# Three early loads change places on two DMA queues of a cross-network kernel

## The chip, the cores and the metric

The kernel runs on one core of a Trainium2 chip. The metric is device time in microseconds of one execution, as the median of several runs. TensorE (PE) does matmuls and loads their weights (PEld), VectorE (DVE), ScalarE (ACT) and GpSimd (POOL) do the rest, and SyncE (SP) only issues DMAs here. DMAs are issued on a queue of the engine that issues them, and the transfers of all queues run on the same 16 DMA engines.

## The reference

Six cross layers on 4096 rows of 416 features (26 fields of 16), all in bf16:

```python
def setup_inputs():
    B, F, D, L = 4096, 26, 16, 6
    Din = min(F * D, 1024)
    return {
        "x0": _w((lambda *s: _rng.normal(s) * 0.05)(B, Din)),
        "ws": _w((lambda *s: _rng.normal(s) * 0.05)(L, Din, Din)),
        "bs": _w((lambda *s: _rng.normal(s) * 0.05)(L, Din)),
    }

def reference(x0, ws, bs):
    x = x0
    for l in range(ws.shape[0]):
        x = x0 * (x @ ws[l] + bs[l]) + x
    return x
```

## The kernel before

**Tiling.** The 416 features are three chunks of 128 (`CH`, index c or m for outputs, k for inputs) and a tail of 32. The 4096 rows are four blocks of 1024 (`SB`, index s), each of two halves of 512 (`H`, index h). Data stand with features on partitions and rows along the free dimension: `x0T_sb` holds the three chunks of x0, `x0t_sb` the tails, where four groups of 256 rows lie on four groups of 32 partitions. The loop at L583 goes over blocks, then layers; `main` (L327) does four matmuls of 32 output columns each for one output chunk m and one input chunk k, `tail_rows` and `tail_outs` (L343, L385) the tail's part, and DVE (L455) adds the bias and multiplies with x0.

**The order of work.** A small planner (`Plan`) keeps one list of operations for each engine in the order in which the code adds them. From the names that an operation reads and writes it derives the semaphore waits. Nothing is reordered: each engine and each DMA queue runs its list in order. A DMA's `writes` key is what later operations wait for.

**The beginning.** The first half of block 0 doesn't come through a transposing DMA. Rows 0 to 511 are loaded as they lie (`load_rows`, two loads of 208 KB into `xin_sb`), turned on TensorE (`turn_rows`, L542) and copied by DVE to `x0T_sb` (L552). TensorE runs 12 filler matmuls (`fill`, L303) before that. Rows 512 to 1023 come through a transposing DMA (`load_transposed(0, H, SB)`, L211), which brings the three chunks but not their tails. The tail inputs of these rows are a load of their own: `xtl_sb`, four groups of 128 rows with 32 features, 64 bytes for each piece, 32 KB in all. `tail_in` (L402) turns the tails of all 1024 rows on TensorE, from `xin_sb` and `xtl_sb`; ACT (L416) and DVE (L420) copy them to `x0t_sb`.

**The weights of layer 0** are three separate loads, one for each input chunk k (104 KB each), so that `main` for k=0 waits only for the first (`weights`, L321). The tail weights of layer 0 are loaded once (26 KB) and replicated on chip (`replicate`, L278). For the later layers `load_main` brings all three chunks in one DMA.

**The first half's first layer** is the one place where the code interleaves by input chunk:

```python
                    for k in CH:
                        for part in range(2) if k == 0 else (None,):
                            for m in CH:
                                main(s, l, 0, m, k, part)
                        if k == 1:
                            tail_in()
                            bias_sums()
                    tail_rows(s, l, True)
```

So TensorE needs, in this order: the rows of `xin_sb`, W0's first chunk, W0's second chunk, the tail inputs, the biases, W0's third chunk, the replicated tail weights, and then the transposed rows 512 to 1023 for h=1.

**The queues before.** SyncE: rows, rows, W0 second chunk, W0 third chunk, transposing load, W1, tail weights of layer 1 (four DMAs), W2 and so on. ScalarE: tail weights of layer 0, W0 first chunk, tail inputs; after these three its compute begins. GpSimd: the biases.

Of the kernel before, what the change touches and what calls it, by code (L numbers as in the profile page):

```python
# [118 lines left out]
def bass_standalone__dcn_v2_cross__recsys_kernel(  # L119
# [6 lines left out]
    B, D = x0.shape  # L126
    L = ws.shape[0]
    NC = 3
    DF = 128 * NC
# [6 lines left out]
    JS = SB // 128  # L136
# [3 lines left out]
    CH = range(NC)  # L140

    with ExitStack() as es:

        def sb(name, shape, dt=BF16):
            return es.enter_context(nc.sbuf_tensor(name, shape, dt))
# [5 lines left out]
        xtl_sb = sb("xtl_sb", [128, JS, DR])  # L151
# [28 lines left out]
        x0_v = x0.rearrange("(j p) d -> p j d", p=128)  # L180
# [6 lines left out]
        def quad(q):  # L187
            return slice(32 * q, 32 * q + 32)
# [5 lines left out]
        def load(queue, dst, src, name, writes):  # L194
            P.add(queue, lambda e: e.dma_start(dst, src), writes=writes, dma=name)
# [13 lines left out]
        def load_transposed(s, a, b):  # L209
            P.add(  # L210
                "sync", lambda e: e.dma_start_transpose(x0T_sb[:, :, s * SB + a:s * SB + b], x0[s * SB + a:s * SB + b, 0:DF]),  # L211
                writes=[("x0T", s, c, h) for c in CH for h in HALVES if a <= h * H < b], dma="x0T%d" % s,
            )
# [21 lines left out]
        load_rows("sync", 0)  # L235
        load_rows("sync", 1)
        load("scalar", wt_sb[quad(0), 0, :], ws[0, DF:D, :], "wt0", [("wtq",)])
        for k in CH:
            queue = "sync" if k else "scalar"
            load(queue, w_sb[:, 0, k, :], ws[0, 128 * k:128 * k + 128, :], "w0_%d" % k, [("w", 0, k)])  # L240
        load("scalar", xtl_sb[:, 4:JS, :], x0_v[:, 4:JS, DF:D], "xtl0", [("xtl", 0)])
        load_transposed(0, H, SB)
        load_main(1)
        load_tail_weights(1, 2, "wt1")
# [548 lines left out]
```

## Time and profile before

| what | us |
|---|---|
| median of 3 runs | 127.68 |
| lowest, highest run | 127.36, 127.82 |
| profiled execution, its own time | 128.1 |
| span of the profiled execution, first to last instruction | 126.8 |
| PE busy | 123.6 (97% of the span) |
| PE weight loads busy | 64.6 (51%) |
| DVE busy | 100.0 (79%) |
| ACT, POOL busy | 43.0 (34%), 41.0 (32%) |

The page gives the busy time of each engine, the chain of work that ended last, the costliest groups of instructions, and the DMA issues with their time to landing. "Q" behind an engine's name (SPq, ACTq) marks the issue of a DMA by that engine's sequencer. Matmuls are pipelined, and a group's busy time says little of what one costs; the distance between the starts of successive groups says more. "x4" at the end of a line means four instructions merged into it.

### The profile page before, as it was taken

How to read it: one execution, taken by the hardware profiler on the slowest of the kernel's cores; microseconds unless marked ns; L12 is line 12 of the kernel's file. 1: busy time of each engine (PE TensorE's matmuls, PEld its weight loads, DVE VectorE, ACT ScalarE, POOL GpSimd, SP SyncE). 2: the span in 40 equal slices, each digit the busy share in tenths (PEclk: the TensorE clock that was granted, in tenths of full speed). 3: DMA queues.
4: the chain of work that ended last, by engine and by line, in shares of the span. 5: the costliest groups of instructions: out<-in, count | busy, mean ns of one | idle time of the engine just before them, and what ended most of it. 6: DMA issues, size and time to landing. Idle time of an engine off the chain costs nothing.

```text
span 126.8 us, 5226 instructions
## 1 busy us (share of the span) xinstructions
PE 123.6 (97%) x2373; PEld 64.6 (51%) x2373; DVE 100.0 (79%) x157; ACT 43.0 (34%) x94; POOL 41.0 (32%) x84
## 2 busy tenths in 40 slices
PE   7999999999999999999999999999999999999992
PEld 5654555555545545545545545555555455455561
DVE  2449779779779779788798797797797797797974
ACT  3324225225205225234213242252222252252910
POOL 6505324134014044053122142251320440543590
DMA  3995999010039596107019695107007990070107
GB/s 108 254 253 157 308 158 158 25 25 0 8 83 130 115 213 70 36 16 274 0 32 207 115 163 99 31 16 252 22 0 173 108 292 5 14 255 10 31 20 249
DMA packets 35013, 14.21 MB, mean 112 GB/s; under 512 B 26186, under 2 KB 34992, under 8 KB 34992
## 3 DMA queue, kind: packets, MB, share of 16 engines
q1 hardware_dynamic: 33536, 13.19, 48.4%
q10 hardware_dynamic: 1424, 0.70, 1.9%
q8 instruction: 18, 0.29, 1.0%
q14 instruction: 3, 0.02, 0.1%
q0 software_dynamic: 32, 0.01, 0.0%
HBM read 3.89 MB, written 3.41 MB: 58 GB/s over the span
## 4 chain that ended last, share of the span: by engine, by line
PE 97%; DVE 0%; issue 0%
PE ps L295 94%; PE ps L303 2%; PE ps L542 1%; DVE o_sb L718 0%
## 5 line engine op out<-in xcount | busy, mean ns | idle before, releaser
L455 DVE SCALAR_TENSOR_TENSOR xT_sb<-ps,cb_sb,x0T_sb 128x512 bf16<-128x512 f32 x114 | 76.8, 743 | 15.6 <-PE ps L295 15.6
L295 PE MATMUL ps<-xT_sb,w_sb 128*32 128x512 bf16 (+1 forms) x1596 | 84.2, 364 | 0.0
L295 PEld LDWEIGHTS ps<-xT_sb,w_sb 128*32 128x32 bf16 x1596 | 40.9, 97 | 37.2 <-issue 4.0
L465 ACT ACTIVATE t_sb<-ps,cb_sb 64x256 f32<-64x256 f32 x46 | 21.6, 470 | 57.2 <-PE ps L295 56.9
L478 POOL TENSOR_TENSOR xt_sb<-t_sb,x0t_sb 128x256 bf16<-128x256 f32 x20 | 13.4, 672 | 66.6 <-ACT t_sb L465 66.6
L430 ACT ACTIVATE xt_sb<-xt_sb 32x256 bf16<-32x256 bf16 x38 | 15.7, 414 | 15.1 <-POOL xt_sb L478 14.9
L295 PE MATMUL ps<-x0T_sb,w_sb 128*32 128x512 bf16 (+1 forms) x348 | 19.2, 369 | 0.0
L432 POOL COPY xt_sb<-xt_sb 32x256 bf16<-32x256 bf16 x38 | 14.9, 393 | 2.4
L455 DVE SCALAR_TENSOR_TENSOR xo_sb<-ps,cb_sb,x0T_sb 128x512 bf16<-128x512 f32 x18 | 12.1, 743 | 2.5 <-PE ps L295 2.5
L295 PEld LDWEIGHTS ps<-x0T_sb,w_sb 128*32 128x32 bf16 x348 | 9.1, 101 | 7.7 <-issue 1.1
L295 PE MATMUL ps<-xt_sb,wt_sb 32*128 32x512 bf16 (+1 forms) x152 | 11.6, 326 | 0.0
L295 PE MATMUL ps<-xt_sb,wc_sb 32*128 32x256 bf16 x76 | 7.3, 268 | 0.0
L295 PEld LDWEIGHTS ps<-xt_sb,wt_sb 32*128 32x128 bf16 x152 | 2.3, 91 | 8.1 <-DVE xT_sb L455 8.1
L478 POOL TENSOR_TENSOR xot_sb<-t_sb,x0t_sb 128x256 bf16<-128x256 f32 x3 | 2.0, 672 | 9.9 <-ACT t_sb L465 9.9
L295 PE MATMUL ps<-w_sb,xT_sb 128*32 128x416 bf16 (+1 forms) x60 | 5.0, 339 | 0.0
L442 DVE SCALAR_TENSOR_TENSOR xT_sb<-ps,cb_sb,x0T_sb 128x512 bf16<-128x512 f32 x6 | 4.0, 744 | 0.8 <-PE ps L295 0.8
L718 DVE TENSOR_TENSOR o_sb<-ps,xr_sb 128x416 bf16<-128x416 f32 x7 | 3.7, 583 | 0.8 <-PE ps L295 0.8
L295 PEld LDWEIGHTS ps<-xt_sb,wc_sb 32*128 32x128 bf16 x76 | 3.9, 93 | 0.2
L303 PE MATMUL ps<-const-bfloat16-1.0 128*128 128x256 bf16 x12 | 2.7, 417 | 0.8 <-PEq L778 0.8
L552 DVE COPY x0T_sb<-ps 128x256 bf16<-128x256 bf16 x6 | 1.4, 292 | 2.2 <-PE ps L542 2.2
L295 PEld LDWEIGHTS ps<-w_sb,xT_sb 128*32 128x32 bf16 (+1 forms) x60 | 2.3, 97 | 1.2
L488 ACT ACTIVATE sS_sb<-ps,cb_sb 128x384 bf16<-128x384 f32 (+1 forms) x5 | 2.7, 629 | 0.0
(48 smaller groups left out, 32.3 us busy)
## 6 DMA issues: line engine op xcount, KB each, us to landing
out_dram<-o_sb SPq DMA_DIRECT2D x2, 832.0 KB, 4.8
w_sb<-in_ws_dram SPq DMA_DIRECT2D x5, 312.0 KB, 3.9
out_dram<-o_sb SPq DMA_DIRECT2D x2, 416.0 KB, 3.2
xr_sb<-in_x_dram SPq DMA_DIRECT2D x1, 832.0 KB, 5.0
xin_sb<-in_x_dram SPq DMA_DIRECT2D x2, 208.0 KB, 2.8
wt_sb<-in_ws_dram SPq DMA_DIRECT2D x4, 104.0 KB, 3.3
out_dram<-o_sb ACTq DMA_DIRECT2D x3, 104.0 KB, 1.9
out_dram<-o_sb SPq DMA_DIRECT2D x3, 104.0 KB, 1.7
```

What stands on the lines that cost most here:

```text
L295: return pe.matmul(dst, lhsT=lhsT, rhs=rhs, start=start, stop=True, skip_group_check=True, tile_position=pos,)
L303: ins = pe.matmul(ps[:, 7, 0:256], lhsT=const[:, 0:128], rhs=const, start=True, stop=True)
L430: fn = lambda e, d=dst, s=src: e.activation(out=d, in_=s, func=ACTF.Copy)
L432: fn = lambda e, d=dst, s=src: e.tensor_copy(out=d, in_=s)
L442: "vector", lambda e: e.scalar_tensor_tensor(out=xj[:, js, c, :], in0=ps[:, bank(h, c), :].rearrange("p (j f) -> p j f", f=128), scalar=cb ...
L455: "vector", lambda e: e.scalar_tensor_tensor(out=dst, in0=ps[:, bank(h, c), :], scalar=cb_sb[:, c, l:l + 1], in1=x0T_sb[:, c, o:o + H], op ...
L465: "scalar", lambda e, p=p, h=h: e.activation(out=dst[p, :], in_=ps[p, T_BANK[h], 0:G], func=ACTF.Identity, bias=cb_sb[p, NC, l:l + 1]), re ...
L478: "gpsimd", lambda e: e.tensor_tensor(out=dst, in0=t, in1=x0t_sb[:, s, 0, :], op=ALU.mult),
L488: fn = lambda e: e.activation(out=o, in_=i, func=ACTF.Identity, bias=b)
L542: ins = pe.transpose(out=psT[:, b, j * 128:(j + 1) * 128], in_=xin_sb[:, 2 * i + j, c * 128:(c + 1) * 128], identity=ident[:, :],)
L552: "vector", lambda e, d=dst, s=src: e.tensor_copy(out=d, in_=s),
L718: "vector", lambda e: e.tensor_tensor(out=o_sb[:, jj, :], in0=ps[:, b, 0:D], in1=xr_sb[:, j, :], op=ALU.mult), reads=[("ps", b), ("xr",)], ...
```

## The change

The tail inputs go from the third place of ScalarE's queue to the third of SyncE's. W0's third chunk goes from the fourth place of SyncE's queue to the third of ScalarE's, and W0's second chunk from the third place of SyncE's to the fourth. The order after it:

| place | SyncE before | SyncE after | ScalarE before | ScalarE after |
|---|---|---|---|---|
| 1 | rows 0-255 | rows 0-255 | tail weights 0 | tail weights 0 |
| 2 | rows 256-511 | rows 256-511 | W0 first chunk | W0 first chunk |
| 3 | W0 second chunk | tail inputs | tail inputs | W0 third chunk |
| 4 | W0 third chunk | W0 second chunk | | |
| 5 | transposing load | transposing load | | |

```diff
@@ -235,10 +235,9 @@
         load_rows("sync", 0)
         load_rows("sync", 1)
         load("scalar", wt_sb[quad(0), 0, :], ws[0, DF:D, :], "wt0", [("wtq",)])
-        for k in CH:
-            queue = "sync" if k else "scalar"
+        load("sync", xtl_sb[:, 4:JS, :], x0_v[:, 4:JS, DF:D], "xtl0", [("xtl", 0)])
+        for k, queue in ((0, "scalar"), (2, "scalar"), (1, "sync")):
             load(queue, w_sb[:, 0, k, :], ws[0, 128 * k:128 * k + 128, :], "w0_%d" % k, [("w", 0, k)])
-        load("scalar", xtl_sb[:, 4:JS, :], x0_v[:, 4:JS, DF:D], "xtl0", [("xtl", 0)])
         load_transposed(0, H, SB)
         load_main(1)
         load_tail_weights(1, 2, "wt1")
```

The number of loads, their sizes and every instruction of the other engines stay as they are.

## The prediction

> **What bounds the kernel now.** I read the chain of waits first. It shows whether a transfer ends anything on the path that sets the end.
>
> ```profile
> 7 pieces in order of time: start us, us, what
> 0.79 0.04 issue
> 0.83 2.72 PE ps L303 x12
> 3.56 0.01 issue
> 3.57 1.50 PE ps L542 x12
> 5.06 119.42 PE ps L295 x2248
> 124.49 0.02 issue
> 124.51 0.59 DVE o_sb L718
> ```
>
> From 0.83 to 124.49 us the chain never leaves TensorE (PE). No DMA is a piece of it. Filler matmuls (L303) run until the first rows land, the turning of the rows (L542) until 5.06, and after that matmul follows matmul. A moved load can change the end only by making TensorE wait where it doesn't now, or by ending a wait that it has.
>
> Second, the timeline of the first 9 us, for the queues that the change touches. Columns: start, duration, engine, line, operation.
>
> ```profile
> 0.80 0.87 SPq L195 DMA_DIRECT2D xin_sb<-in_x_dram  x2
> ...
> 1.25 0.45 ACTq L195 DMA_DIRECT2D w_sb<-in_ws_dram  x1
> ...
> 1.71 0.91 SPq L195 DMA_DIRECT2D w_sb<-in_ws_dram  x2
> 1.72 0.46 ACTq L195 DMA_DIRECT2D xtl_sb<-in_x_dram  x1
> ...
> 2.66 1.64 SPq L211 DMA_TRANSPOSE x0T_sb<-in_x_dram  x1
> ```
>
> The third and fourth places of SyncE's queue are issued at 1.71 and (by a closer look) 2.19 us, the third of ScalarE's at 1.72. Third, the DMA issues one window at a time, whose last figure is the time from issue to landing; I add it to the issue.
>
> ```profile
> w_sb<-in_ws_dram SPq DMA_DIRECT2D x1, 104.0 KB, 3.1
> xtl_sb<-in_x_dram ACTq DMA_DIRECT2D x1, 32.0 KB, 4.3
> ...
> w_sb<-in_ws_dram SPq DMA_DIRECT2D x1, 104.0 KB, 3.7
> x0T_sb<-in_x_dram SPq DMA_TRANSPOSE x1, 4.6
> ```
>
> So W0's second chunk (w0_1) lands at 1.71 + 3.1 = 4.8 us, the tail inputs (xtl) at 1.72 + 4.3 = 6.0, W0's third chunk (w0_2) at 2.19 + 3.7 = 5.9, the transposed rows 512 to 1023 at 2.66 + 4.6 = 7.3. Last, narrow timelines of TensorE, for when each is first wanted.
>
> ```profile
> 6.04 0.16 PEld L295 LDWEIGHTS ps<-x0T_sb,w_sb 128*32 128x32 bf16 x4
> ...
> 6.25 0.56 PE L295 MATMUL ps<-x0T_sb,w_sb 128*32 128x512 bf16 x4
> ...
> 6.64 0.38 PE L295 MATMUL ps<-x0T_sb,w_sb 128*32 128x512 bf16 x4
> ...
> 6.86 0.10 PEld L295 LDWEIGHTS ps<-ident,xtl_sb 128*32 128x32 bf16 x2
> ...
> 7.38 0.34 PEld L295 LDWEIGHTS ps<-x0T_sb,w_sb 128*32 128x32 bf16 x12
> ...
> 8.69 0.34 PEld L295 LDWEIGHTS ps<-x0T_sb,w_sb 128*32 128x32 bf16 x16 [0.21 <-issue]
> ```
>
> These are the weights for k=1 (6.04, first matmul 6.25), `tail_in` (6.86), k=2 (7.38), and the second half of the rows (8.69). The slack today is 6.04 - 4.8 = 1.2 us for w0_1, 6.86 - 6.0 = 0.8 for xtl, 7.38 - 5.9 = 1.5 for w0_2, and 8.69 - 7.3 = 1.4 for the transposed rows. None of the four is late, so there is nothing to win from landing one earlier.
>
> **The change, part by part.** No instruction is added or removed; three of eight early loads change places.
>
> *Issue time.* SyncE issues xtl (0.46 us, from ScalarE's row) where it issued a weight chunk (0.43). What stands behind it there is the transposing load at 2.66, then w1 at 4.35 and the later weights: each 0.03 us later, with 1.4 us of slack at the transposing load and 10.76 - (4.35 + 3.9) = 2.5 us at w1, whose first use is the loading of xT weights at 10.76. Without that cover it would cost 0.03 us. ScalarE issues a chunk in 0.45 in place of 0.46; behind it stand its table load (2.21) and the replica of the tail weights (3.72), wanted at 8.14. Cost: 0.
>
> *Tail inputs, third on SyncE.* They take the place from which w0_1 landed at 4.8. They are 32 KB against 104, but in 64-byte pieces. ScalarE's queue moved 622 packets, most of them these, in the window 3.5 to 7.3 for 14.8% of 16 engines, i.e. 0.148 x 3.8 = 0.56 us for each engine; that is the most they can hold up one engine. Landing between 4.8 and 4.8 + 0.56 = 5.4; I take 5.0. Wanted at 6.86, as now. Gain 0, since TensorE has no wait there.
>
> *W0's third chunk, third on ScalarE.* Issue 1.72. Bounds: 1.72 + 3.1 = 4.8 (a chunk's quickest) and 1.72 + 4.3 = 6.0 (the place's own figure today). Wanted at 7.38, so at least 1.4 us of slack. Cost 0.
>
> *W0's second chunk, fourth on SyncE.* This is the one load that comes closer to its use. Issue about 2.19. Lower bound: 2.19 + 3.1 = 5.3. Next: 2.19 + 3.7 = 5.9, what the fourth place gave w0_2. Upper bound: 2.19 + 4.3 = 6.5, the slowest of these loads. Against 5.9 speaks that its queue now holds 208 + 208 + 32 = 448 KB ahead of it, where w0_2 had 520, and that no small packets run beside it by then. Estimate from third place plus the small packets: 4.8 + 0.56 = 5.4. I take 5.5, between these two and nearer the lower. That leaves 6.04 - 5.5 = 0.5 us to the weight load and 0.7 to the matmul. Cost 0; from a landing of about 6.1 on it costs what it is late. At 6.5 the first matmul starts near 6.5 + 0.15 (one weight load), 0.4 us late. TensorE's in-order work behind that wait is all there is: `tail_in`, the bias sums, k=2, tail rows.
>
> The Trainium skill, "DMA: Bandwidth & Descriptors", section Queues, rings and completion order, says that on each engine a queue's descriptors are taken in order while the queues that have work alternate. By that rule w0_1 waits for all the small tail pieces and w0_2 runs beside them; the sum would still be 0, with the landing at 5.4 rather than 5.9.
>
> *The transposing load.* The same bytes stand ahead of it on the 16 engines, in the same number of SyncE issues; 7.3 plus or minus 0.3 (the gap between the two estimates above), wanted at 8.69. Cost 0.
>
> *TensorE's only early wait for a load* is on the second pair of rows, issued at 1.26, ahead of everything that moves. It lands about 1.26 + 2.9 = 4.2, and turning resumes then. What runs beside its last packets is the end of W0's first chunk in both kernels. Bound either way: 0.06 us, the break between the two runs of six turning matmuls.
>
> **Sum.** 0.0 us, from -0.06 to +0.4 on these rows without what follows below. Against the profiled execution: span 126.8, its own time 128.1, so 1.3 us lie around the span; both stay. That execution is 0.4 us above the median 127.68 of the three runs, so I forecast the median itself and not 128.1: **127.65 us**.
>
> **Rivals.**
> (a) *Slower: w0_1 comes late and the fast matmul rate with it.* The rows above show that groups of 512 columns start 0.39 us apart from 6.25 to 6.64 and 0.22 apart from 6.64 to 6.86; before that, groups of 256 columns start 0.21 apart (5.61 and 5.82 in a closer look). TensorE ran at about half rate until some 6.6 us, although the windows show a granted clock of 1.00 throughout. If w0_1 lands after 6.1, TensorE idles shortly before that step. Had the step needed the 3.0 us of work since its last wait (3.57 to 6.6) and to start over, it would cost 0.4 + 3.0/2 = 1.9 us: 129.6. If the step keeps its time, only 0.2 to 0.4: 127.9 to 128.1. For it: 5.9, the fourth place's landing, is only 0.2 from the deciding point. Against: the bytes ahead are fewer, and the idle stretch is short. The Trainium skill, "TensorE: Matmul & The Clock Gate", Part 1, ties the step to a busy window of about 3.4 us; by it a spoilt window would cost up to 3.4/2 = 1.7 us on top of the stall, 129.8. The trace agrees with a step in rate, not yet with any window.
> (b) *Faster: the profile flatters the old order.* xtl has the least slack, 0.8 us, and its landing is the latest of the small loads. In runs without a profile it may miss 6.86; the new order would remove that. The three runs spread from 127.36 to 127.82, so the typical price is up to 0.3: 127.36. It would take a usual lateness of 0.7 us more to reach a real gain, 127.0. Against: no wait at `tail_in` at all in the trace.
> (c) *The step in rate moves by itself*, with when the engine started rather than with the loads: each 1.3 us earlier or later is worth 0.65, so 127.0 or 128.3. Against: the three runs hold within 0.46, i.e. 0.9 us of step.
> (d) *The change doesn't do what it says:* the 16 engines are full (248 to 368 GB/s from 3.5 to 4.25 us), and xtl lands near 6.0 as before. Time: 127.65 all the same, since nothing waits for it.
>
> **How the numbers follow.** A measurement of this kernel can tell about 0.5%, 0.64 us, from no change. Forecast with earlier tail inputs 0.47, (d) 0.10, both within 0.5%. (a) 0.18, of which 0.13 with the late step (slower) and 0.05 within. (b) 0.13: 0.07 faster, 0.06 within. (c) 0.12: 0.06 faster, 0.05 slower, 0.01 within. Together faster 0.13, same 0.69, slower 0.18. The forecast's own range is that of the runs, 127.3 to 127.9; letting in the near parts of (a), (b) and (c) gives 126.9 to 128.5, which leaves out about 0.12 above and 0.07 below.
>
> **What would show it.** Right: the chain is still TensorE alone from 0.83 on; xtl lands near 5.0 (below 5.5), w0_1 between 5.3 and 5.9; the first k=1 matmul starts near 6.25, `tail_in` near 6.86, k=2 near 7.40. Wrong: idle time of the weight loads before 6.1 put down to the DMA of w_sb, half-rate spacing (twice 0.21 us at 512 columns) lasting beyond 7 us, or the first update of layer 0 (DVE L455, 8.61 us now) more than 0.3 us off its place.

## The result, and the profile after

The changed kernel takes 128.09 us in the median of 8 runs (127.99 to 128.65) against 127.48 (127.14 to 127.82, 8 runs) for the kernel before: a ratio of 1.0054, 95% interval 1.0034 to 1.0074. It is slower by about 0.6 us. The profiled execution is the longest of the eight: 128.65 us, span 127.4.

The chain of waits of the changed kernel (start, duration, what; its L294 is L295 of before):

```profile
by line: PE ps L294 92.7%; DMA w_sb<-in_ws_dram 3.6%; SPq L195 1.0%; DVE o_sb L717 0.5%; issue 0.3%
12 pieces in order of time: start us, us, what
...
1.71 0.43 SPq L195
2.14 0.04 issue
2.19 4.63 DMA w_sb<-in_ws_dram
6.81 0.14 issue
6.95 118.08 PE ps L294 x2230
...
```

Where TensorE alone made the chain before, it now begins on SyncE's queue: the rows, the tail inputs (issued at 1.71), then W0's second chunk, issued at 2.19 and landed at 6.81. TensorE's own work enters the chain only at 6.95, with the first matmul of k=1. The timeline of TensorE around that point shows the wait itself (the last column is idle time before the group and what ended it):

```profile
4.30 0.51 PE L541 MATMUL ps<-ident,xin_sb 128*128 128x128 bf16 x6
4.74 0.84 PE L294 MATMUL ps<-x0T_sb,w_sb 128*32 128x256 bf16 x24
6.95 0.40 PE L294 MATMUL ps<-x0T_sb,w_sb 128*32 128x512 bf16 x4 [1.37 <-DMA w_sb<-in_ws_dram]
```

The 24 matmuls of k=0 are over in 0.84 us here. In the profile of before they began at 4.99 and lasted until k=1 began at 6.25; the twelve of k=1 follow in the same line, with no idle time:

```profile
4.99 2.25 PE L295 MATMUL ps<-x0T_sb,w_sb 128*32 128x256 bf16 x36
```

So in this execution TensorE was at its full rate more than 2 us earlier, won about 1 us by it, and lost that and more in 1.37 us of waiting. The DMA issues of the changed kernel between 1.6 and 2.6 us, the last figure being the time from issue to landing:

```profile
w_sb<-in_ws_dram ACTq DMA_DIRECT2D x2, 104.0 KB, 3.9
xin_sb<-in_x_dram SPq DMA_DIRECT2D x1, 208.0 KB, 3.0
w_sb<-in_ws_dram SPq DMA_DIRECT2D x1, 104.0 KB, 4.6
xtl_sb<-in_x_dram SPq DMA_DIRECT2D x1, 32.0 KB, 4.6
bsa_sb<-in_bs_dram POOLq DMA_DIRECT2D x1, 4.9 KB, 5.0
```

The tail inputs land at 1.71 + 4.6 = 6.3, no earlier than before (6.0), and the second chunk at 2.19 + 4.6 = 6.8, where it landed at 4.8. By the trace's single increments of its semaphore, six of the sixteen shares had come by 5.34 us and the other ten came between 6.24 and 6.81.

### The profile page after: what moved, and what is told of

It reads as the page before. It is cut to its first block, busy times and chain, and to the rows that moved or that the text cites. A ratio compares the mean times of both kernels' runs of the same rounds, so it can differ in the third digit from the quotient of the medians.

```text
span 127.4 us, 5226 instructions
## 1 busy us (share of the span) xinstructions
PE 122.8 (96%) x2373; PEld 64.0 (50%) x2373; DVE 100.0 (78%) x157; ACT 42.9 (34%) x94; POOL 40.9 (32%) x84
## 4 chain that ended last, share of the span: by engine, by line
PE 93%; DMA 4%; SPq 1%; DVE 0%; issue 0%
PE ps L294 93%; DMA w_sb<-in_ws_dram 4%; SPq L195 1%; DVE o_sb L717 0%
## 5 line engine op out<-in xcount | busy, mean ns | idle before, releaser
L294 PE MATMUL ps<-xT_sb,w_sb 128*32 128x512 bf16 (+1 forms) x1596 | 84.2, 364 | 0.0
L294 PEld LDWEIGHTS ps<-xT_sb,w_sb 128*32 128x32 bf16 x1596 | 40.9, 97 | 37.2 <-issue 4.0
L294 PE MATMUL ps<-x0T_sb,w_sb 128*32 128x512 bf16 (+1 forms) x348 | 18.7, 358 | 1.4 <-DMA w_sb<-in_ws_dram 1.4
L294 PEld LDWEIGHTS ps<-x0T_sb,w_sb 128*32 128x32 bf16 x348 | 8.7, 96 | 8.8 <-issue 2.5
L294 PE MATMUL ps<-xt_sb,wt_sb 32*128 32x512 bf16 (+1 forms) x152 | 11.6, 326 | 0.0
L294 PE MATMUL ps<-xt_sb,wc_sb 32*128 32x256 bf16 x76 | 7.4, 268 | 0.0
L294 PEld LDWEIGHTS ps<-xt_sb,wt_sb 32*128 32x128 bf16 x152 | 2.3, 91 | 8.1 <-DVE xT_sb L454 8.1
L294 PE MATMUL ps<-w_sb,xT_sb 128*32 128x416 bf16 (+1 forms) x60 | 5.0, 339 | 0.0
L294 PEld LDWEIGHTS ps<-xt_sb,wc_sb 32*128 32x128 bf16 x76 | 3.9, 93 | 0.2
L294 PEld LDWEIGHTS ps<-w_sb,xT_sb 128*32 128x32 bf16 (+1 forms) x60 | 2.3, 97 | 1.2
```

The lines of the kernel that those rows point to most:

```text
L294: return pe.matmul(dst, lhsT=lhsT, rhs=rhs, start=start, stop=True, skip_group_check=True, tile_position=pos,)
```

## The experiments

The kernel before runs beside each of them. All change the list of early loads or what runs beside it. The position of a load in the list is that of its queue. In the expectations "second chunk" and "third chunk" are W0's; in the edits, shortened here to the order of the queues where that says more, they are W0[1] and W0[2].

**e1: the changed kernel again.** No edit.

> The changed kernel unaltered, for a second profile beside the first. If the late landing of W0's second chunk is what costs (both theories below), TensorE waits again before the first matmul of k=1, for the DMA of w_sb, and the time is 1.003 to 1.007 of before. If the wait in the first profile was an accident of that execution, k=1 starts within 0.1 us of the end of k=0 and the time is still 1.003 or more.

Measured: ratio 1.0035 (1.0014 to 1.0056), 12 runs. The second profile has the same wait:

```profile
4.58 0.84 PE L294 MATMUL ps<-x0T_sb,w_sb 128*32 128x256 bf16 x24
6.69 0.61 PE L294 MATMUL ps<-x0T_sb,w_sb 128*32 128x512 bf16 x8 [1.27 <-DMA w_sb<-in_ws_dram]
```

The chunk landed at 6.55. The wait is no accident of one execution.

**e2, e3, e4: one move at a time.** e2 only exchanges the two chunks on SyncE's queue, e3 only moves the tail inputs, e4 is the change with the second chunk put back ahead of the tail inputs.

```diff
 # e2: tail inputs stay third on ScalarE
-sync: rows, rows, W0[1], W0[2], transposing
+sync: rows, rows, W0[2], W0[1], transposing
 # e3: W0[2] stays on SyncE
-sync: rows, rows, W0[1], W0[2], transposing      scalar: tail weights, W0[0], tail inputs
+sync: rows, rows, tail inputs, W0[1], W0[2], transposing      scalar: tail weights, W0[0]
 # e4: against the changed kernel
-sync: rows, rows, tail inputs, W0[1], transposing
+sync: rows, rows, W0[1], tail inputs, transposing
```

> Only W0's second and third chunk change places on SyncE's queue (third chunk third, second chunk fourth); the tail inputs stay third on ScalarE's. Theory place (the fourth place of SyncE's queue, next to the transposing load, lands too late for k=1 whatever stands third): second chunk lands at 5.9 or later, ratio 1.003 to 1.006. Theory small pieces (the tail inputs' 64-byte pieces on SyncE's queue hold up what stands behind them): second chunk lands by 5.9 and the ratio is 0.999 to 1.001.

> Only the tail inputs move: third on SyncE's queue, with W0's second chunk fourth and its third chunk fifth, ahead of the transposing load. Theory place: the second chunk is one place further from the transposing load than in the change and lands near 5.4, ratio 0.999 to 1.002. Theory small pieces: as late as in the change, ratio 1.004 to 1.007.

> The change with the tail inputs and W0's second chunk exchanged on SyncE's queue: second chunk third, tail inputs fourth, third chunk third on ScalarE's. Theory place: second chunk lands by 5.0 and k=1 waits for nothing; the tail inputs land late in its stead, 6.0 to 6.8, wanted between 5.4 and 6.9, so the ratio is 0.998 to 1.002. Theory small pieces: the second chunk is now ahead of them, so also 0.998 to 1.002, but the transposing load lands as late as in the change (7.8 and more, against 7.3).

Measured: e2 1.0020 (0.9997 to 1.0042), second chunk at 6.17; e3 1.0010 (0.9985 to 1.0034), at 5.57; e4 0.9987 (0.9964 to 1.0009), at 5.17, with the tail inputs at 6.08 in its stead. Undoing the one exchange of places (e4) takes the loss back: its interval lies below those of the change and of e1. By time alone e2 and e3 can't be told from before, but the profile of e2 has the wait, and that of e3 hasn't:

```profile
6.31 0.83 PE L295 MATMUL ps<-x0T_sb,w_sb 128*32 128x512 bf16 x12 [0.56 <-DMA w_sb<-in_ws_dram]
```

The chain of e4 has no DMA in it again:

```profile
6 pieces in order of time: start us, us, what
0.79 0.04 issue
0.83 2.72 PE ps L303 x12
3.56 1.43 PE ps L542 x12
4.99 118.74 PE ps L295 x2244
...
```

The second chunk is late where it is the last of the three loads W0[1], W0[2] and tail inputs to be served (change, e2) and not where it is the first (before, e4). In e3, where one of them stands ahead and one behind, it lies between. e2 also tells that the small pieces of the tail inputs needn't stand ahead of it. The transposing load landed at 7.38 in e4, against the 7.8 that the small-pieces theory wanted.

**e5, e6: the transposing load moved away.** In the change and in e2 the second chunk stands directly in front of the transposing load. In both kernels this load now goes behind W1:

```diff
-        load_transposed(0, H, SB)
         load_main(1)
+        load_transposed(0, H, SB)
```

> The changed order of the early loads, with the transposing load of rows 512 to 1023 issued behind W1 and no longer directly behind W0's second chunk. Theory neighbour (the transposing load's packets hold up the landing of the load directly in front of it): second chunk lands by 5.4 and k=1 starts when k=0 is through, 5.4 to 6.3; TensorE may wait for the transposed rows instead (landing near 8.2, wanted 7.9 to 8.7), ratio 0.996 to 1.001. Theory load (the second chunk is late because of the bytes ahead of it on both queues): it still lands at 6.2 or later, ratio 1.003 to 1.007.

> The order of before, with the transposing load behind W1. Theory neighbour: W0's third chunk, then in front of W1, lands by 5.4 and not at 5.9, the tail inputs near 5.3 and not at 6.0; k=1 starts as before and the tail inputs can't be late in executions with an early full rate: ratio 0.996 to 1.000, unless the transposed rows come late for the second half (up to +0.3 us). Theory load: landings as in before, ratio 0.999 to 1.003.

Measured: e5 1.0030 (1.0004 to 1.0056), second chunk at 6.66, with W1 between it and the transposing load:

```profile
2.19 4.47 DMA w_sb<-in_ws_dram
6.66 0.14 issue
6.79 2.35 PE ps L295 x61
```

The neighbour theory falls; "load" holds. e6 1.0036 (1.0014 to 1.0057), a loss that neither theory had: the tail inputs landed at 6.61, later than in the order of before, and `tail_in` waited. The weight loads of TensorE in e6 show it:

```profile
6.65 0.10 PEld L295 LDWEIGHTS ps<-ident,xin_sb 128*32 128x32 bf16 x2 [0.56 <-DMA xtl_sb<-in_x_dram]
```

In addition the transposed rows came at 8.47 there, and the second half of the rows began at 8.51.

**e7: the kernel before again, one execution.**

> The kernel before, for a second profile. If its scatter (127.1 to 128.3) is the time at which TensorE's rate doubles, then the time is 121.65 us after the first matmul of k=1 (plus up to 0.2 if that matmul is still slow) as in all five profiles so far, and an execution near 127.3 shows the doubling before 5.0 us, one near 128.1 at 6.0 or later. If the scatter comes from the DMAs, TensorE waits for a DMA in the slower one.

Measured: 127.58 us. TensorE waits for none of the loads behind the rows:

```profile
5.06 1.61 PE L295 MATMUL ps<-x0T_sb,w_sb 128*32 128x256 bf16 x36
```

The groups of k=0 start 0.19, 0.17 and then 0.11 us apart: the rate doubles near 5.4 us, where it doubled near 6.6 in the first profile of before. The expectation named 5.0 and 6.0 for executions of 127.3 and 128.1, and this one lies between in both. k=1 starts at 5.86, and 5.86 + 121.65 = 127.51: the execution time follows the start of k=1. In the change (6.95), e1 (6.69), e2 (6.31), e3 (5.89), e4 (5.66), e7 (5.86), e8 (6.35) and e13 (6.42) the span ends 120.4 us after it, alike to 0.03 us. That makes the start of k=1 the thing to watch.

**e8: second chunk on ScalarE's queue.**

```diff
-sync: rows, rows, tail inputs, W0[1], transposing      scalar: tail weights, W0[0], W0[2]
+sync: rows, rows, tail inputs, W0[2], transposing      scalar: tail weights, W0[0], W0[1]
```

> The change with W0's second and third chunk exchanged between the queues: tail inputs third and third chunk fourth on SyncE's, in front of the transposing load; second chunk third on ScalarE's. Theory neighbour: second chunk lands by 5.4, the third chunk at 5.9 to 6.8, wanted between 6.5 and 7.4: ratio 0.995 to 1.000. Theory load: the bytes ahead are those of the change, so the second chunk lands at 6.0 or later: 1.002 to 1.006.

Measured: 1.0022 (1.0001 to 1.0043), second chunk at 6.21, k=1 at 6.35:

```profile
6.35 0.83 PE L295 MATMUL ps<-x0T_sb,w_sb 128*32 128x512 bf16 x12 [0.78 <-DMA w_sb<-in_ws_dram]
```

Third place on the other queue is as good as fourth on this one: both other loads still run ahead of it or beside it. "Load" again.

**e9, e10: the bias load.** Why is the last of these loads so late? In the trace one 832-byte packet that starts between 4.1 and 4.6 us takes 1284 ns (change), 732 (before), 936 (e1), 726 (e2), 762 (e4), 921 (e5), 729 (e6), 1178 (e8), 500 (e3) and 479 (e7); its like take 39. The biases' packets run at that time, so they are moved (with the clearing of their tile on DVE, which goes ahead of them):

```diff
-gpsimd: biases
+sync: ..., transposing, biases, W1
```

> The changed order, with the 4.9 KB bias load taken from GpSimd's queue and issued on SyncE's, behind the transposing load. In every profile so far one 832-byte packet that starts between 4.1 and 4.6 us, while the bias load's packets run, takes 0.5 to 1.3 us. Theory bias load (it stalls one engine, and the last of the early loads waits for that engine): no such packet, the second chunk lands by 5.6 and k=1 starts by 5.8 or at the end of k=0; the biases themselves may come late, near 7.2, wanted about 1.5 us after the start of k=1. Theory last in line (the second chunk is served after the other two early loads, whatever runs beside it): it lands at 6.2 or later, ratio 1.002 to 1.007.

> The order of before with the bias load moved in the same way. Theory bias load: the third chunk and the tail inputs land by 5.6 rather than at 5.9 to 6.3; ratio 0.997 to 1.002, since TensorE then waits at most for the biases. Theory last in line: landings as before, 5.9 to 6.3; ratio 0.999 to 1.004.

Measured, with 4 runs each: e9 1.0084 (1.0055 to 1.0113), e10 1.0075 (1.0048 to 1.0102). What they lose beyond the order of their loads I put down to the late biases (landed at 8.08 and 7.81 us, with the sums that need them at 8.17 and 7.90; k=2 starts at 8.27 and 8.00, where it started at 7.92 in the change and at 7.40 in before), more than I had allowed. The question itself is answered by the landings: a packet of 598 ns in e9 and of 607 in e10 is still there, and the second chunk lands at 6.30 in e9, the tail inputs at 6.37 in e10. So the late landing and the long packet don't need the biases beside them.

**e11: the change without the load of the tail inputs.**

```diff
-src = xin_sb[:, j, DF:D] if j < 4 else xtl_sb[:, j, :]
+src = xin_sb[:, j % 4, DF:D]
```

The load itself and the wait for it are left out as well, so the tails of rows 512 to 1023 are those of other rows.

> The changed order without the load of the tail inputs; the tails of rows 512 to 1023 are taken from the rows of the first half instead, so this load and its 512 pieces are left out. Theory last in line: the second chunk is now third on SyncE's queue, beside the third chunk only, and lands near 5.2 as in the swapped order, k=1 starts at the end of k=0; ratio 0.997 to 1.000. Theory slow engine (the second and third chunk share an engine that stalls for about a microsecond, small pieces or none): 6.0 or later, ratio 1.000 to 1.004.

Measured: 0.9974 (0.9952 to 0.9997). With one load fewer the median shows no loss. But the profile, of an execution of 128.25 us, has a packet of 1254 ns, and the second chunk, third on its queue, lands at 6.09; k=0 was slow enough there (k=1 at 6.38) to hide it. So the ratio speaks for "last in line", the landing for "slow engine": the stall comes without the small pieces, too, and being early in line makes it only less likely that the chunk is what it hits.

**e12, e13: GpSimd's replica copies.** They run from 3.83 to 4.93 in the change, across the start of the long packet. ScalarE makes them instead, in the change (e12) and in the order of e4 (e13).

```diff
-for g, eng in ((1, "gpsimd"), (3, "scalar"), (2, "gpsimd")):
+for g, eng in ((1, "scalar"), (3, "scalar"), (2, "scalar")):
```

> The changed order, with the two replica copies of the tail weights that GpSimd does (3.8 to 4.95 us) given to ScalarE, so that GpSimd touches no memory while the early loads land. Theory GpSimd (its copies hold up the writes of one DMA engine): no packet of 0.5 us or more starts between 4.0 and 4.6, the second chunk lands by 5.6, ratio 0.998 to 1.001. Theory last in line, stall from elsewhere: a packet of 0.6 to 1.3 us at the same time, landing 6.2 to 6.8, ratio 1.002 to 1.006.

> The swapped order of e4 (second chunk third on SyncE's queue, tail inputs fourth, third chunk third on ScalarE's) with the same replica copies on ScalarE. Theory GpSimd: the tail inputs land by 5.6 as well and an execution with an early full rate waits for nothing, ratio 0.995 to 0.999. Theory last in line: tail inputs at 6.0 or later, ratio 0.997 to 1.001.

Measured: e12 1.0042 (1.0024 to 1.0061), a packet of 781 ns, second chunk at 6.18. e13 1.0005 (0.9980 to 1.0029), tail inputs at 6.01. The GpSimd theory falls. No kernel of this study that does the whole work beats the kernel before: e4, the best, can't be told from it.

What the orders did, with the profile's landing of the second chunk, its start of k=1, and the ratio. In the first three rows k=1 starts when k=0 is over, in the last three when the chunk is there. The landings are of single executions, and the intervals of the ratios are some 0.004 wide, so neighbours in the table can't be told apart by time:

| kernel | served ahead of or beside the second chunk | lands | k=1 | ratio |
|---|---|---|---|---|
| before (e7) | tail inputs beside | 4.84 (4.89) | 6.25 (5.86) | 1 |
| e4 | W0[2] beside | 5.17 | 5.66 | 0.9987 |
| e3 | tail inputs ahead | 5.57 | 5.89 | 1.0010 |
| e2 | W0[2] ahead, tail inputs beside | 6.17 | 6.31 | 1.0020 |
| e8 | tail inputs, W0[2] beside | 6.21 | 6.35 | 1.0022 |
| change (e1) | tail inputs ahead, W0[2] beside | 6.81 (6.55) | 6.95 (6.69) | 1.0054 (1.0035) |

## Why the prediction was wrong

*The step that failed* is the landing of the second chunk, "I take 5.5, between these two and nearer the lower", and with it the term "Cost 0". It measured 6.81, 6.55 and, with the transposing load moved away, 6.66, beyond even the upper bound of 6.5. These three profiles are of executions among the longest of their kernels; the median of the change stands for a landing near 6.2 (below), inside the bounds and still 0.7 us behind 5.5. The rows for the right answer were on the page: of the three loads that share the engines, the last landed at 6.0 us in before, and by making the second chunk the last one the change gave it that landing or a later one. I argued it down with bytes ahead and with a share of 16 engines. But a landing is counted at the last of sixteen shares, and one share alone can be late: in e10 fifteen of the second chunk's had come by 4.67 us and the last at 5.38, in e5 fifteen by 5.96 and the last at 6.66. In 12 of the 15 profiles one packet takes 0.6 to 1.3 us just then. In the change it is over at 5.46, and from 5.51 to 5.98 fourteen more 832-byte packets start, one at a time, as if a single engine had its part of both chunks still to do; in before the last such packet of these loads starts at 5.27. The upper bound missed because it took the slowest issue-to-landing of a single profile (4.3 us); 4.6 (change) and 4.9 (the tail inputs in e6) occur.

*The second fault* is in the slack. I took 6.04 as the time at which the chunk is wanted, from an execution in which TensorE ran at half rate until 6.6. In e7 it is wanted at 5.75, in the change and e1 it would have been at about 5.3 and 5.1 (the start of the last group of k=0, where the weights of k=1 were loaded in before and e7). I had this as rival (c), a step that moves by itself, and gave it a price of its own; I didn't let it meet rival (a). Together they are the result: however early the full rate comes, k=1 can't start before the chunk has landed.

*Rival (a)* had the mechanism, TensorE idle for the DMA of w_sb, and too small a chance (0.18). Its dear branch, 129.6 with a fast rate that starts over, didn't occur: after the stall the groups of 512 columns start 0.21 us apart in the change and in e1. But there the full rate had come before the stall, so what a stall ahead of the step would do stays open. Its cheap branch, 127.9 to 128.1, is where the median lies, in part by luck: it counted 0.2 to 0.4 us onto 127.65, where 0.6 onto 127.48 was measured. The section of the Trainium skill on the clock gate ("TensorE: Matmul & The Clock Gate", Part 1) would have warned of the second fault, since it calls the window free-running and the transition variable from run to run. The profiles agree, with a wider spread than the ±500 ns that it gives: the step lies before 4.4 us in the change and near 6.6 in before. The 129.8 that I drew from its window didn't occur, and wasn't tested either: a stall of 1.4 us behind the step didn't take the full rate back.

*The sum by the measured terms.* A profiled time less its start of k=1 is 128.65 - 6.95 = 121.70, 128.42 - 6.69 = 121.73, and 127.58 - 5.86 = 121.72 for e7. The medians 128.09 and 127.48 so stand for starts of k=1 near 6.4 and 5.8, and the chunk lands 0.14 us ahead of k=1 where k=1 waits for it. The difference of 0.6 us is, by this reckoning, what the late chunk costs. The scatter of the kernel before (127.03 to 128.31 in most runs of this study) would follow as well, since 1.3 us in time is 2.6 us in the place of the step; that is argued from two profiles of it and not shown.

*Right, point by point.* Only a new wait on TensorE could matter, and in the change and e1 it waits for none of the other moved loads: SyncE's issue of the transposing load came 0.07 us later (0.03 forecast), its landing at 7.93 and 7.60 (7.0 to 7.6 forecast, so late in one of the two) is still ahead of the second half at 9.23 and 8.97. *Wrong without a cost:* the tail inputs were to land at 5.0 and landed at 6.29 and 6.01, so rival (d) was true as well; the third chunk landed at 6.27, outside 4.8 to 6.0, wanted at 7.9. By the rule of the Trainium skill on rings ("DMA: Bandwidth & Descriptors", Queues, rings and completion order) I had 5.4 for the second chunk. The table agrees with its order of service, but the landings of the change, e1 and e5 are 1.1 to 1.4 us later than I drew from it.

*Open:* what makes the long packet from about 4.2 us on, and how much of the late landing is due to it. Not the transposing load's place (e5), the biases (e9, e10), the small pieces (e11) or GpSimd's copies (e12): the packet is there in each of them. The packets and shares above make the stall the likely reason for the last share of the change and e5, but it isn't the whole answer: e13 has no such packet, and its tail inputs, last in line, land at 6.01 all the same. Forcing the step of TensorE's rate to one time wasn't tried.

## What to carry to other kernels

Among loads that are in flight together, put the one that is wanted first at the head of its queue, and reckon the landing of the last from the last landing of the set in several profiles, not from bytes. Slack that is read from one profile holds only if the consumer's time doesn't move: here it moved by a microsecond from one execution to the next. A new floor under the start of a stage takes the fastest executions away first (the lowest run is 127.99 us here against 127.14) and can hide in a slow one, so compare medians over many runs.

## What the runs showed of the hardware that was not expected

*TensorE's rate.* Windows of one microsecond show a granted clock of 1.00 throughout, in the half-rate stretch too. Of before:

```profile
5.00:6.00 1.00, 1.00 (x21) 0.76 (x24) 0.39 (x2) 0.00 (x0) 0.21 (x1) 1.00 1.17 212
```

and of e7, in the same stretch:

```profile
5.00:6.00 1.00, 1.00 (x30) 0.80 (x32) 0.46 (x3) 0.00 (x0) 0.21 (x1) 1.00 1.20 158
```

The columns are the stretch, its length, busy time of PE, PEld, DVE, ACT and POOL with the number of instructions, the granted clock, the DMA share and GB/s. Both are full of matmuls, 21 against 30 of them, with 1.00 in the clock column. But this 1.00 is no measurement: the traces of before and e7 hold no record of the granted clock, and the view then shows 1.00. Six of the fifteen traces have one, and it begins at the step: at 4.11 us (e8), 4.68 (e2), 4.78 (e5), 5.12 (e6), 5.25 (e10) and 5.57 (e9). In e9 the groups of k=0 start 0.19 and 0.20 us apart up to 5.59 and 0.11 apart from there. Without such a record the distance from start to start tells the rate, and the clock column doesn't.

*Busy engines that move little.* In the change, the same stretch has the engines at a share of 1.32 and 139 GB/s, against 1.17 and 212 in before (e7, above, lies between):

```profile
5.00:6.00 1.00, 0.58 (x24) 0.29 (x12) 0.31 (x2) 0.00 (x0) 0.21 (x1) 1.00 1.32 139
```

By the trace, 346 packets of 256 bytes, the transposing load's, start between 5.20 and 5.83 us. Of these, 328 are over by 5.85, and the other 18, which take 0.41 to 1.02 us, all end between 6.20 and 6.25, as if they waited for one engine. The ten late shares of the second chunk come right behind them, from 6.24 on; in e5, where the transposing load doesn't follow it directly, only one share comes after 6.0. So the transposing load seems to hold up many of the shares, but not the last one, on which the landing hangs. The DMA share alone doesn't tell waiting from traffic: it was 1.25 with 292 GB/s in before from 6 to 7 us, and is 1.32 with 139 GB/s here.
